# Filter rotation and first filter DFT in plain float32, in a recurrence and long-convolution kernel

## The chip, the cores and the metric

The kernel runs on one core of a Trainium2 chip. The time is that of one execution on the device, in microseconds (us); lower is better. TensorE (PE) multiplies matrices, VectorE (DVE) and ScalarE (ACT) read its results from PSUM, GpSimd (POOL) works on SBUF alone, and SyncE (SP) issues all DMAs. PEld stands for PE's weight loads.

## The reference

Two stages follow each other: a gated recurrence along the sequence, and a block that convolves with a filter through Fourier transforms. B is 4, S is 6272, D is 256, all in float32.

```python
sig = 1.0 / (1.0 + np.exp(-f_logit))
f = lower_bound + (1.0 - lower_bound) * sig
for t in range(S):
    h = f[:, t] * h + (1.0 - f[:, t]) * x[:, t]
    y[:, t] = h
proj = y @ w_proj                                  # [B, S, 3 D]
x1, x2, x3 = proj[..., :D], proj[..., D:2 * D], proj[..., 2 * D:]
H = np.fft.rfft(filter_fft, n=S, axis=0)[None]
x2_conv = np.fft.irfft(np.fft.rfft(x2, n=S, axis=1) * H, n=S, axis=1)
out = (x1 * x2_conv * x3) @ w_out
```

## The kernel before

S is split as 128 x 49 (M and Q), so that a transform along the sequence is two rounds of matmuls with small tables: a first DFT over the 128 positions of one residue, and a second one over the 49 residues. Before that, each of the 49 rows r of the sequence has to be turned cyclically by its own number of positions. For the batches this comes with the projection; for the filter it is done with matmuls against a shifted identity ("rotation").

The preparation, which `prepare` records, has these steps for the filter:

- `ff` (line 622): 13 loads of up to four rows (512 KB each), 7 into X2, the others into Hu and HA.
- `fr` (line 631): for the groups not in PLAIN = (0, 2, 4, 6, 8, 10), a copy on ACT or POOL that rounds the group to float32r, PE's fast form of float32, into one of the two buffers `afs` (the second is Hx).
- `rot` (line 639, matmul on line 637): each row times the shifted identity `rot`. Groups in PLAIN are rotated as plain float32 where they landed, with the identity read as float32; the others as float32r from the buffer.
- `f2` (line 640): the eviction of a group of rotated rows to the tile f2, in float32r, by ACT or DVE (lines 291 and 296 of the helper `copy`).
- `FF1` (line 663, matmul on line 661): the first DFT. A unit is 8 columns of pairs of channels, 16 units in all; each column is one matmul with 128 x 128 of f2 as weights and the table D1r as the moving operand. D1r is stored twice side by side, so that a matmul moves 256 columns in float32r, of which half are not used. A unit is two steps of four matmuls.
- `afs` (line 666): the eviction of half a unit, 512 elements per partition, to one of two buffers. `mX` (line 670) copies its first column.
- `FF2` (line 681, matmul on line 679): the second DFT of a unit; `hw` (line 684) evicts the spectrum, `hst` (line 688) stores it to DRAM, from where each batch loads it back (`H`, line 772).

All of FF1 needs all of f2. `hgrn` for batch 0 runs between the steps of the filter: loads of f_logit and x in 13 chunks (`load`, line 334, through four sets of buffers), sigmoid (`sig`, 337) on ACT, a product (`u`, 339) on POOL, transposes (`su`, 353, on line 351) on PE, a gate (`f`, 364 or 366) and the scan (372) on DVE. A chunk has two `su`, one for each half of the channels, and its buffers are free for the chunk four places later once both are done.

Then, for each batch: the projection to the convolved part (`P`, line 725), the first and second DFT (737 and 795), products with the spectrum (816 and 825), the inverse (835 and 869), the gates x1 and x3 (400) and the output projection (887). The next batch's recurrence runs between these steps.

Nothing is scheduled at run time. Every step is recorded with the tags that it reads and writes and a cost that a planner used offline; the string ORDER then gives, for each step in turn, its engine and its PSUM bank, and `emit` issues them in this order. So each engine, and SP's queue of DMAs, has a fixed sequence, and an instruction that waits holds back all behind it on its engine. WARM steps are matmuls without use of their result (two of float16 with 256 columns each, line 603), which fill gaps of PE.

Of the kernel before, what the change touches and what calls it, by code (L numbers as in the profile page):

```python
# [64 lines left out]
class Plan:  # L65
# [68 lines left out]
    "EuACnQEaMEkWCZYCbCEvYCoIClUElGCjSE6AEmOEoQFMgCmECiYE7YEpIFNgCkCEwUEqICwWExEE0SCxGEyMCqQFXgETYE1CC1WErgCpYCrAEPYFWg"
    "E2KE8UEbYCNgFEAE/QC2OC3SFhgFAAFFYE9MCuWFggC4CCdgFBICvGAGgFOACzWE+MFGSCyYC0GC5YFPYFJQFHKC+UFqgFKAFIKEngC6WC/EFrgC7G"
    "FQUFLICtgDASFYADHWFRMAnRDBCFTQFSMDIGDCYDFSFZYF0gFUADQWB8gDGCFVIDDUFiAC9gDKSDEMFaQDRGDJYFjYDLCDXWFbIDVUALADNgDOSDYO"
    "DWEF1gFcIDPCFdWD7YFsADTUMTgDSYFeOCcgFkQDUEFtYDgSFfOFlAFnUDhCFmIDeWMfgFoEC8gDaSD3YDfGCMgFpMFuQEDYDbCMggDlWDZYCsgEfY"
    "F2AFvIDMgDnUDiYDmGEzYF+gDjSFwIDoEBtYFxWDkCE3YJQUFyODqQDpYJSEF3YFzOJRVDrAEHYJVSJWTJTFDsgF4QF7WJYDF5IDtgDuUJUYF8OJXC"
    "F6IF/gMUgJaTF9OGigJbQJZYJcDGIRJdIG0gDvEGQWJeYGJBG9gGUUGRGGGQDdgGVEGKSGHIMhAGAWGLCGOQGBOGMUGPAGrgGCSDcgGNEMrgGEQGDK"
    "MVAGSWGFAGWSGTOJfVGXCJgXJkRJlQJhFJmJGYTJnAJivGeVGZDJoYJpQJjYGfNJqXJuRJsHGaSJrIJwBGjWGbCJtYGcUGnuJvRGdEJzTJxpJ0QGoY"  # L140
    "J1DJ4XJyYJ2IGgSGsUJ6HGhKJ3YG1QGwEGluJ5XG5AHGSGkYJ7vGxYGmYJ9VHQgHHCJ+RGusJ8YGpWJ/FHMSGvYGqGG3oGtYHZgG+UG2YG6YKABHIW"
    "HNKG4YGyQHJGHAsHKSGzAKBYHigG7WHLCMsgHCsHBYKCQG/YMiYKEAHORHRTHDYHrgHPJMtAKDQHVrHERHTDKHVKFoG8GHWYHUYKITHFJKGYKMQKJF"
    "HaWKOAKKrH0UHeuKLYH4QHSYH+gH1EHbYHXSHcuHfYMuYHjUHYCHlsH5AHdYIHgH2WHgSH3GHnsHmYHkYHsQMWYHhCH6WHuoHoYIQgHpUH7GH/SHwo"
    "HvYHqEH8WKNQIBCH9OIIUHxYHtYIZgIDqIAYIRRIKEICYHyWITBKPoIEYKRTHzGIMsKQYKSUIiQKTDILYIsgIFWINYIjAKUsKWTIVpKVYKXVIGGMXQ"
    "IJYI1gKZFIUYKYLIWYIaWMYAMbUIeGMZIIOSM3gMcEM4gKbXISYIPCIfYMdMIXQKdHImSIYAIcuMjUInCIkQKaYMkMIdYJHgIoWIlAI+gKcTMlMIbY"
    "KgSIpGItQKerKiCIqUMnWIvoKfYIxAKhTNDgMoGIyYIgRIrMNEgIwYM5AMpOKlQI2UIhBKjrMvWI3YKnAIuYI6sKkYMzSM6YMwGKmRNQgI4EMxOKqQ"
    "I7YNPgM0CIzUKsAM1KM7WI0EJAYI5YNFAKrUKopKvSKtsKpYM8GM/QKuYKxCJIUNGYM9ONbgNAAI8SNcgJMEMygNBIKwXJKEK0WI9CI/UJLYKyvK2G"
    "K1RJBsKzYNHSK3BNRAK5WJDsJCYK4YNLQNICNlgK7OJEYJFUNMANSYNmgNJKK6XJGEK+WNdANNIK/SNTTJJYLAGNeYK8vNXQNUDLBqK9YLDVNvgNYA"
    "NVLLEWLCYNwgLFFLIXLKHLJVJNYLGuNnANfSLLtLHYLNWNZILMYLOXLPGNiUNgCLQvN5gJOQNjENhKLRYNoYNOgRtXJPAN6gRuWM+gNkMRvHLSQRwG"
    "LXSNxALTINpUNsWNqENyYLYKLUQODgNtGOEgNrMLZSLVAMeYNuOLcULWgLaCNaYNzQLdMLbgRyXN0ALhSR0HN1IN7AN2ULmWONgN3ELiKN8YOOgLeQ"  # L150
    "OFAN4MLjSLfALnOOGYLrULkCN9QLsMOAWN+ALoSMqAOXgN/IOYgOBGLlgOHULpCNKgOCOLwQOPAOKSLxILtWUwgOLCOQYLqgOIEOMKLyQLuGOJMLzA"
    "L1WORSOZAL2OL0gRzROSCOaYLvgL6UR1BNWYOTKOUQMaYObWM2YU8gL7MOVAL3SOcGNCAOdOOeUMmAOWIVJgL8WL4CVIgUxgOfMMEQL9GU9gOgML/S"
    "LggMFIOxUL5gL+gMAKOhQOyEOtWOiAOvTOuOUyAO3QOwDOjWO4AOnTUzYOkOVKAO1QOoDOpWO2AOlUU+AOzQOmMOrSU/YO0AMBUOsKOqGMJQMCEVLY"
    "O5WMKIO9SMDgO6GMGUO+CMOQPDWMPIMHEPHuO7QRxYR3SO8AO/UPFuPIYR2YR4TPAEMLQR5KPGYPtgR6DPBUPLWMMAR7YPCMPbSPNuPTUPdCPEYR8Q"
    "PXEPMYPPuPOYPJRR+APlVPKBPYYPVsPQYP2gR9QSBXPmFPRRR/oPWYSDHPjVSAYPfqPSBPcYSCQPUYPeYSGXSEASHUPgYSIPPkFPpSPnQSJsPZWPoA"
    "SFYQIgPqKSKYP/gPuUPaGPhQPysPrSP3WPiAPsKPzYSLVPwsP5GP4YQRQPvYSNFP6YQJSQSAP7uPxYQbgQAVMIgSMUQEFSQQP8YSOsQNCP0WQkgSSI"
    "SPYSRUP1GQCtQFYSVQSWTSXAQTWSTsQDYP9QQUGSYrSUYQBYSaVQtgQLqSZYQOYQVTP+AMNgQGWScFQWLQMYSbSQHGQcQQKYQ2gSdCQXUQgoQPWSeY"
    "QYESfTQeoQhYQQGQZRQlUShDQaJQfYRJgQ3WQnsQpEQdYQ/QQmYQ7GQiSQqYQ5GRAIQoYQuUQjCU0WQysQwERBQQvYU1GQxYU4SQzYRCAU2OQrUVUg"
    "RSgU5CVAQVVgQsEQ6YU6KQ0WRbgVBARDUQ1GSgSVCISkTREEQ8YRKWSiqSlQSmDROuSjYSpRSnARFUSrBSqQSoYRMuRPYRGESuTVERSsoQ4YRNYSwD"
    "RHUVggSvWRIMVFBStYSzXVhgSxGRTTRkgVGJVWAQ9VSyYRVLVMQQ+FRLYRXrVXYS0TS1HRQVVNAS2rRYYS4SRRFVOIS5XS3YS9US6CRWYRcVS/ES7v"  # L160
    "VQSReFRgtS8YVYQVsgVRCVtgS+XViARUYVSKRhYTCWRfYRZUVZATAvTDTRaETHSVaITBYTIXTEGVjYVcUTJCTFrRlQV4gVdETKvTGYTMWV5gRpARno"
    "TNTTLYU7gTOGRmYTRXRdYRqYTSSTTHVeMRoYVkQVuARiWTPrVlATWUTUqTQYVvYRjGTXTVmITVYTbSTYEVoWTdCVngTcRVpOTZDWCgVwUV6ATaYVqO"
    "WDgTgQRrSVxETepTiAVrYV0WVyMRsCTfYV7YThQWMgV1GTlRTjoTmVTnBMQSV2OTkYToFTqUTrRMRCTpYTsEMSgTvSU3ATtpWNgV8UVPYWEATuYTwK"
# [814 lines left out]
```

## Time and profile before

| | |
|---|---|
| median of 3 runs | 460.49 us (459.06 to 460.7) |
| the profiled execution | 461.27 us, span 459.3 us |
| PE busy | 444.2 us (97%), 6009 matmuls |
| DVE, ACT, POOL busy | 402.4, 406.7, 306.0 us |
| DMA | 121.40 MB, mean 264 GB/s |
| mean granted PE clock | 0.999 |

The busy time of an engine is the time in which at least one of its instructions ran. Matmuls follow each other in a pipeline, so the mean duration of one (0.2 to 0.4 us) is longer than the distance from one start to the next. In rows in order of time, "x8" is a number of instructions, the first number the start and the second the length of the merged piece, in us from the start of the span; what is in brackets is idle time before it and what ended it. SPq rows are the issues of DMAs. Rows of lines 291, 293, 296 and 298 are evictions by the helper `copy`, to be told apart by their tiles.

### The profile page before, as it was taken

To read this page: it belongs to the slowest core of one execution; us is meant where nothing else is said; L and a number is where in the kernel's file an instruction comes from. 1 tells how busy PE (TensorE), PEld (TensorE's weight loads), DVE (VectorE), ACT (ScalarE), POOL (GpSimd) and SP (SyncE) were. 2 spreads that over 40 slices of the span, in tenths; PEclk is the share of its full clock that TensorE was granted. 3 is DMA by queue.
4 is the path that set the end of the run, shared out by engine and by line. 5 is a ranking of instruction groups with operands and counts; after the bars stand their busy time and mean duration, and the time that the engine had idled before them with its cause. 6 is when DMAs were issued, how large, how long until landed. Compare 5 with 4: busy or idle time off the path is not lost.

```text
span 459.3 us, 14604 instructions
## 1 busy us (share of the span) xinstructions
PE 444.2 (97%) x6009; PEld 346.6 (75%) x6009; DVE 402.4 (88%) x450; ACT 406.7 (89%) x563; POOL 306.0 (67%) x282
## 2 busy tenths in 40 slices
...
GB/s 321 387 349 330 316 340 407 314 143 253 272 310 248 337 326 298 106 233 265 279 229 296 284 294 350 101 320 326 226 244 304 287 229 26 241 185 186 31 289 290
DMA packets 45154, 121.40 MB, mean 264 GB/s; under 512 B 4384, under 2 KB 8352, under 8 KB 45088
## 3 DMA queue, kind: packets, MB, share of 16 engines
...
HBM read 86.12 MB, written 31.98 MB: 257 GB/s over the span
## 4 chain that ended last, share of the span: by engine, by line
PE 66%; DVE 15%; ACT 6%; DMA 5%; issue 5%; POOL 2%; ACTq 0%; SPq 0%; DVEq 0%; POOLq 0%
PE PS L400 15%; PE PS L725 9%; PE PS L835 9%; PE PS L887 7%; PE PS L351 6%; DVE HA L372 6%; PE PS L795 6%; PE PS L737 6%; DVE ys L875 4%; DMA FL<-in_f_logit_dram 3%; PE PS L869 2%; PE PS L661 2%; DVE PP L816 2%; DMA X<-in_moe_filter_fft_dram 1%; ACT fTs L364 1%
## 5 line engine op out<-in xcount | busy, mean ns | idle before, releaser
L339 POOL TENSOR_TENSOR XT<-XT,FL 128x1024 f32<-128x1024 f32 (+1 forms) x49 | 109.8, 2245 | 53.6 <-ACT FL L337 36.5
L372 DVE TENSOR_TENSOR_SCAN HA<-fTs,HA,PS 128x512 f16<-128x512 f32 (+1 forms) x96 | 112.9, 1201 | 2.8 <-ACT fTs L364 2.0
L400 PE MATMUL PS<-HA,W 128*128 128x490 f16 (+1 forms) x416 | 103.8, 367 | 1.0 <-DVE HA L372 0.3
L825 POOL TENSOR_TENSOR PP<-HA,Hu 98x1008 f16<-98x1008 f16 x39 | 81.8, 2106 | 6.8 <-ACT HA L291 2.7
L291 ACT CAST HA<-PS 128x1024 f16<-128x1024 f32 (+1 forms) x98 | 79.1, 833 | 4.2 <-PE PS L737 2.2
L431 POOL TENSOR_TENSOR zt<-gx 128x490 f16<-128x490 f32 (+1 forms) x43 | 52.4, 1223 | 41.1 <-ACT gx L291 16.6
L816 DVE TENSOR_TENSOR PP<-PS,Hu 98x1008 f16<-98x1008 f32 x57 | 66.7, 1199 | 0.6 <-ACT gx L293 0.5
L875 DVE TENSOR_TENSOR ys<-PS,zt 128x1024 fp32r<-128x1024 f32 (+1 forms) x52 | 58.7, 1149 | 8.5 <-PE PS L869 6.7
L887 PE MATMUL PS<-Wo,ys 128*128 128x256 f32 x392 | 58.1, 293 | 0.6 <-DVE ys L875 0.3
L364 ACT ACTIVATE fTs<-PS,cc 128x512 f32<-128x512 f32 (+1 forms) x84 | 55.3, 679 | 2.8 <-PE PS L351 2.1
L835 PEld LDWEIGHTS <-PP 98*128 98x128 f16 x1024 | 50.2, 97 | 9.8 <-issue 1.7
L400 PEld LDWEIGHTS <-W 128*128 128x128 f16 x416 | 34.4, 97 | 30.6 <-issue 7.8
L835 PE MATMUL PS<-VV,PP 98*128 98x98 f16 x1024 | 55.9, 206 | 0.3
L887 PEld LDWEIGHTS PS<-Wo,ys 128*128 128x128 f32 x392 | 49.7, 188 | 6.0 <-DVE ys L875 1.5
L293 ACT ACTIVATE gx<-PS 128x490 f32<-128x490 f32 (+1 forms) x87 | 50.1, 583 | 4.5 <-PE PS L400 3.1
L291 ACT CAST Th<-PS 128x784 f16<-128x784 f32 x59 | 48.4, 820 | 4.1 <-PE PS L835 3.1
L337 ACT ACTIVATE FL<-FL 128x1024 f32<-128x1024 f32 (+1 forms) x49 | 49.4, 1010 | 1.8 <-DMA FL<-in_f_logit_dram 1.6
L351 PE MATMUL PS<-iden,FL 64*128 64x64 f32 x736 | 42.7, 231 | 2.5 <-ACT HA L293 0.9
L725 PE MATMUL PS<-W,HA 128*128 128x256 f16 x392 | 44.6, 273 | 0.2
L725 PEld LDWEIGHTS <-HA 128*128 128x128 f16 x392 | 43.0, 142 | 1.2 <-issue 0.2
L351 PEld LDWEIGHTS PS<-iden,FL 64*128 64x128 f32 x736 | 31.7, 138 | 16.0 <-issue 2.6
L422 DVE TENSOR_TENSOR zt<-PS,gx 128x490 f16<-128x490 f32 (+1 forms) x61 | 38.8, 647 | 1.6 <-PE PS L400 0.9
(128 smaller groups left out, 741.8 us busy)
## 6 DMA issues: line engine op xcount, KB each, us to landing
...
```

What stands on the lines that cost most here:

```text
L291: nc.scalar.copy(dst, src)
L339: op("u", {"POOL": 0.1 + 0.553 * nb}, lambda e, xt=xt, ft=ft: nc.gpsimd.tensor_tensor(xt, xt, ft, op=AOP.mult), r=[("ft", k)], w=[("xt", k)])
L351: nc.tensor.transpose(bank(pb)[:, at[p] + j:at[p] + hn:nb], src[ps, j, cols], iden[ps, ps])
L364: nc.scalar.activation(fT, sT, AF.Identity, scale=by, bias=1.0)
L372: nc.vector.tensor_tensor_scan(h, fT, bank(pb)[:, 512 - hn:512 + hn], init, op0=AOP.mult, op1=AOP.add),
L400: nc.tensor.matmul(PS[:, p, 0:n], W13[:, kh, js], HA[:, HB[kh] + t0:HB[kh] + t0 + n], start=(kh == 0), stop=(kh == 1))
L725: nc.tensor.matmul(pp[:, r - r0, :], column(HB[kh], q_of(r)), W2[:, kh, :], start=(kh == 0), stop=(kh == 1))
L816: nc.vector.tensor_tensor(pr, px.unsqueeze(1).broadcast_to([TB, 2, UE, 63]), hh, op=AOP.mult)
L825: nc.gpsimd.tensor_tensor(pr, spec[:, o, :, 1:64].unsqueeze(1).broadcast_to([TB, 2, UE, 63]), hh, op=AOP.mult)
L835: nc.tensor.matmul(PS[:, ib + o, pr * TB:(pr + 1) * TB], PP[:TB, k, o, n, 2 * pr:2 * pr + 2, :], v[:TB], start=(n == 0), stop=(n == 1))
L875: nc.vector.tensor_tensor(late["ys"][:, yk, :, 0:rn * 128], PS[:, cb:cb + 2, 0:rn * 128], late["zt"][:].rearrange("p k r m -> p k (r m)") ...
L887: nc.tensor.matmul(po[:, i, :], late["ys"][:, yk, kh, i * 128:(i + 1) * 128], Wo[:, kh, :], start=(kh == 0), stop=(kh == 1))
```

## The change

- PLAIN and the seven `fr` copies are gone. Every group of the filter is rotated where its load put it, with both operands declared plain float32; `rot` and f2 are float32 tiles instead of float32r.
- D1r is a float32 table of 128 columns, stored once. A unit of FF1 is one step of eight matmuls with 128 columns, both operands plain float32, and one eviction of 1024 elements per partition; FF2 and mX of a unit wait for that one.
- The planner's costs for the two steps are other ones, and ORDER is a new string for the whole kernel (2371 steps instead of 2410: 7 `fr`, 16 `FF1` and 16 `afs` fewer).

The sequences that ORDER spells out, for the stretch that is edited (numbers are groups, units and chunk halves; `load` 0 is the first of f_logit):

- SP before: ff 3, 2, 0, 1, 4, 7, 6, wcol, ff 5, 12, 8, 9, 10, 11, load 0, 1, 4, 2, 3, 5, 6, 7, wl0, load 8, hst1, ... After: load 0, ff 0, wcol, ff 5, 6, 2, 4, 3, 1, 7, 8, 9, 12, 10, 11, load 1, 2, 4, 3, 5, 6, 7, wl0, load 8, ...
- PE before: 10 warm, rot 3, warm, rot 2, 0, 4, 1, 6, warm, rot 7, warm, rot 5, two warm, rot 8, 9, 10, warm, rot 11, two warm, rot 12, two warm, FF1 (halves) 1, 0, 3, 2, FF2 0, FF1 4, FF2 1, FF1 5, 6, su0, FF1 7, su1, ...
- PE after: 11 warm, rot 0, four warm, rot 2, 6, 4, 5, 1, two warm, rot 3, 7, 8, 9, 10, 11, warm, rot 12, warm, FF1 0, 1, FF2 0, FF1 2, FF2 1, su0, FF1 3, su1, FF2 2, FF2 3, su2, ...
- `afs` evictions: 23 on ACT and 9 on DVE before; 12 on ACT and 4 on DVE after.
- From the first P on, PE has the same steps in both, in a similar sequence. Some evictions and short copies of the batches change between ACT, DVE, POOL and SP.

```diff
-PLAIN = (0, 2, 4, 6, 8, 10)
 ORDER = (
...
-    FF1 = [("FF1", u, h) for u in range(NU) for h in range(2)]
+    FF1 = [("FF1", u) for u in range(NU)]
...
-        rot = tmp.tile([128, 256], F32R, name="rot")
+        rot = tmp.tile([128, 256], F32, name="rot")
...
-        D1r = tmp.tile([128, 2, 128], F32R, name="D1r")
+        D1r = tmp.tile([128, 128], F32, name="D1r")
...
-        f2 = head.tile([128, NEP * PF + 16], F32R, name="f2")
+        f2 = head.tile([128, NEP * PF + 16], F32, name="f2")
...
-            if g in PLAIN:
-                fr, ft, turner = raw, et, rot[:].bitcast(F32)
-            else:
-                j = g // 2 % 2
-                fr, ft, turner = afs[j].rearrange("m r i k -> m (r i k)").rearrange(
-                    "m (r d) -> m r d", d=D), [("af", j, 0), ("af", j, 1)], rot
-                op("fr", {"ACT": 0.08 + 0.214 * rn, "POOL": 0.1 + 0.235 * rn, "DVE": 0.1 + 0.267 * rn},
-                   lambda e, raw=raw, fr=fr, rn=rn: copy(e, fr[:, 0:rn], raw[:, 0:rn]), r=et, w=ft)
-
-            def rotate(e, pb, r0=r0, rn=rn, fr=fr, turner=turner):
+            def rotate(e, pb, r0=r0, rn=rn, raw=raw):
                 pr = PS[:, pb:pb + 2].rearrange("m a (r e) -> m (a r) e", e=256)
                 for r in range(r0, r0 + rn):
-                    nc.tensor.matmul(pr[:, r - r0, :], turner[:, m0_of(r):m0_of(r) + 128],
-                                     fr[:, r - r0, :], start=True, stop=True)
-            rt = op("rot", {"PE": (0.43 if g in PLAIN else 0.12) * rn}, rotate, r=ft + ["rot"], take=2)
+                    nc.tensor.matmul(pr[:, r - r0, :], rot[:, m0_of(r):m0_of(r) + 128],
+                                     raw[:, r - r0, :], start=True, stop=True)
+            rt = op("rot", {"PE": 0.216 * rn}, rotate, r=et + ["rot"], take=2)
...
-            for h in range(2):
-
-                def first(e, pb, f=f2, j=u * UE + h * 4):
-                    pa = PS[:, pb:pb + 2].rearrange("m a (i c) -> m (a i) c", c=256)
-                    for i in range(4):
-                        nc.tensor.matmul(pa[:, i, :], f[:, (j + i) * PF:(j + i) * PF + 128],
-                                         D1r[:].rearrange("m x k -> m (x k)"), start=True, stop=True)
-                f1 = op("FF1", {"PE": 0.475}, first,
...
-                op("afs", either(512), lambda e, pb, af=af, h=h: copy(
...
+            def first(e, pb, f=f2, j=u * UE):
+                pa = PS[:, pb:pb + 2].rearrange("m a (i c) -> m (a i) c", c=128)
+                for i in range(UE):
+                    nc.tensor.matmul(pa[:, i, :], f[:, (j + i) * PF:(j + i) * PF + 128],
+                                     D1r[:], start=True, stop=True)
+            f1 = op("FF1", {"PE": 0.9}, first,
+                    r=[("f2", g) for g in range(13)] + ["D1r", "f2e"], w=[("FF1", u)], take=2)
+            op("afs", either(1024), lambda e, pb, af=af: copy(
+                e, af, PS[:, pb:pb + 2].rearrange("p a (i r k) -> p r (a i) k", r=2, k=64)),
+               w=[("af", u % 2)], src=f1)
```

More of the change, by code (lines that the diff above doesn't have):

```diff
@@ L134 @@
[L134 to L163, printed above, removed]
@@ L189 @@
[L189 to L192 removed]
+    "AAYDJgA+gAMYABIAiQACIADgAxWBNgAuSBQgAkWAZQBEgAnUBKgA9YANIAaQBHgAyQAmVAfWAcUA/QBBgDLAAEYBTgAqTBWgAtXAgSBZgAlTAPIAOA"
@@ new lines @@
+    "BFSBAAATYAVYBRVBigBGCBcgBLQBSFBOTBMABCWARIApQBfgBDGAhQBPLBIRDKgDVgBJBASIDhgBUTDWgBXWBVLDigBaQDtgBYGAUIDugBdSBbAAWY"
+    "BeKAFgBgUAXYAbRBhEBjWAjRBkOAQABnQDMYBsSBoABtKBqWBzUBpYBrOAYYDXABvQDNSB0MDjAB4WBuYDYYDOCBwIDRUB5GD5gDPKB2QDSED6gB7W"
+    "B3ADkYDTMDZSB8GAeRAdRDaKAsQDvADdWDbKB1YDlQEFgDeGDwYEGgB/SDfODmAAIADpUCACDnICEWERgB6YD7AESgDqMAoRDoYAGgArTCCQCFGCBY"
+    "DrMDxSCDACGYDyKD8YD1UEHACLQDzKEbgEcgAHAAvXD2MCHWCMAEIYD3MCIGD9QEBSD+IETACQUElgCNYD/IEmgECCEUYEJWCREEDKENQEKGCOUEwg"
+    "AKAEOIEvgCTSCSYCPEBlYCJgELOCUCCcUEPIEdAEVSCdMEYQEWCEeYCXWE5gEnAEZIE6gCKgEXKCYGEfUEoYAJAEaICaWEgEEiSCbGEhMCfQFEgFDg"
@@ new lines @@
+    "CgACZYEpWBxgCeYEjKCjUExACigEkKDsgCoQCkEChgEyYEqOCpACmSErOEsUE7ACrQFOgEtMD0YC0WFNgCsAClYEuMBygCqYE8YCnCEzQC1OEAgE0A"
+    "E2SFFAE1ICvULsgE3CFGYDUgE9QCwEE4KFAWALACyUL5gFBOC7SCWgCzECxYE+IC2YL4gBmYB9gE/IC8CFHUB+gEMYLtgFPAC3SFCOFIEDAQCtgC4C"
+    "FJMDgYFXgFKWDBAFQYC6gC+SFLOD4YAwUC/CIpUDQYFMODDQC9YIrEEEYIqSDEAIuVDCYDcYIsqIvUIwFItYEQYFRWFUQDHSFSOMEgFVAFTOFYgIzV"
+    "DICFWII0WIxsFbQGWgI2GI1NIyYDGgFtWMFgFcADFgFhSCVgFuGFpUFiKF7gL6AFrWC5gLuAL7YFjSFsOCugFqEFnQFkKI4XI3YGNgFZUI6HFoIFlS"
+    "FaEFdWFmKMGAFfQFeOGEgFvTFgAI5XFwDI9RI7vI+QJCSI8YJAAFxWJEKI/BF3UFyOJDQJBYF4EFzRJHTJFoF0BF8WJGYF1UGAuJJDJISF2EJMTJKq"
@@ new lines @@
+    "JNRGBYJODJRXF+uJLYJPBGFUJTHF5SGOQJQYF/YGpgF6KGJEJSWGSIGfSF9YJUuGGYJWVGKYGgCGHsJXRJVYGCWJYFGlSGIYGDGGQoGXUGTYGygJZB"
+    "GhWGmKGRYGLQGiGGZsGjSGMAGPYG7gJaYGUWGkCGbsGaYJbQGYYJdAGnRGqTGcYHEgGoJGVGJcQGsLJgRJeoJhXGtYGdSGurJfYJjHJiBJlQGeCGzW"
+    "GvYJnIGrYHXgHNUG0YG1uJkYGwSHOEHRQG3uG2YLvYGxCG8UHSAHAsG4YHggHPWG5SHQGG+sHBYHFQG9YHGYG6CMHYHTWHHoG/YHpgHCUHUGHYSHJo"
+    "HIYHDEHVWJmQHaCHqUHWOHKYHygJooHhRHbYHsEHcqJpYHLWHjBH7QHMGHlpHdYJqTHZYIFgJrUHkYJsDHeWHmYH8AJtsJvTHusJuYJwSHfGLwQHiY"
+    "IOgJyCHrYJxLHtYHzWHvYLxAL0UH3GLyIHnSMQgL1EMRgJ0XHoCJzYIXgL2MHwQJ2HH/SHxAH4YH1uL8UIACH9QL9MH2YIBWH+AJ1SL+MH0YIggJ5T"
@@ new lines @@
+    "ICGIGQJ3qJ7DIDUMAWIIoJ4YIKAJ6TMcgMBGILYH5RMdgIEMIJYMSAMCOIPUH6BJ+QJ8rMIWIHYKAAMTYITsJ9YMMSMJGJ/RMogIREMKOKDQIUYMpg"
+    "MNCIMUKFAISYMOKMUWINEKEQMVGKBpMYUMeAKGoKCYKISM0gIQYIZYMWOKHYM1gIhQMZEMfYKJTKKCMaMIlAIVWIjAIWGKLrIYUIkYMqAKMYMgSIcs"
+    "MkQMhCIasM+gIdYKNVMlAM/gMrYKOWKPFKSXMiKIbYIeUKUHM2AKTXKQuKXSKVvKRYImYIfEKYTMmIKWYMsWKZCKcVMtGKarMwQM3YKeFMuOKbYKdU"
+    "NIgMxAKhVNJgKiTKjFKfsKmXNAAKnWKkrKgYMjYM4UMyIKlYKoHIiYM7SNBYM5ENTgKpGInQM6MNSgM8CMngRGWIoARHXM9KKqYRJHKrQRIGNCUKsI"
+    "NKAKwSNFWNDEKxKNLYKtQNcgNGGNdgNEMKySKuANHOK1UKzCKvgNMQK2MK0gRLWNNAK6SRNGNOINUANPUK/WNmgNQEK7KNVYNngK3QNeALzgMvgNRM"
@@ new lines @@
+    "K8SK4ALAONfYLEUK9CK5gNWQLFMNZSNXALBWNwgNaCNYINxgMzgNgULCGNbKLJQNoANjWLKILGSUJgNhENpYL/gNkGNiMLLQLHCNlOLMALOSMLYNqU"
+    "L3YLPKLNgLTQNrEMDYMXgRMXNyANsMNtSROHNzYUWgNuCN0WLUIUVgLQUN1GMPAN2OMbYLVQLRENvKN3ULWALdWUhgN4MLYSN5MUKgULALeOUigOKU"
+    "K+gOIQLSgLZKOLELIgN6WLXgOJALDgOGTN7OUXAOQQOHLUYYOEWORAN8UOFOOMQN9EOASONIUjAOOUOBCUkYOCWOPEN+SODOLaUN/CUMYLiWLbEOSS"
+    "LjOOWQLcgOTCLfUOXILnSLgEOcWLoKOUQOeuRKYRQSOVAOYUOguRRTRPYOfYOZELkQRTLOhYPGgRSCOaUOkWLlAObMO0SOmuOdYOsURUYO2CRVQOwE"
+    "OouOnYOiRRXAO+VOjBOtYOusOpYPPgRWXOlYOxYRaQO/FOqRRYvOvYRcAO8VRZYO4qOrBRbQO3YPYgRfUO9FRdoRgXO5YPCSRhMReYRiHPAQOyWO1Y"
@@ new lines @@
+    "PBAPhgPDKRjYPHUOzGO6QPLsPESPQWO7APFKPMYRkVPJsPSGPRYPqQPIYRmFPTYPiSPrAPUuPKYP0gPZVLhgRlUPdFRpQPVYRnsPmCPNWP9gRrARoY"
+    "RqTPOGPbtPeYRuRRvURwBPsWRsrPcYPWQRxsPtGRtYPaYRzVQGgRyYPkqPnYPuTPXAPfWPvDR1NPlYP1QPgGPwSP5oPjYQPgR0VPxCPoWR2tP6YR4T"
+    "PpGP3oR3YPyRP+UR6DQQWPzJP4YQCEQigQAsQYQP2YQUGQDYP7SQSGQZIQBYQHUP8CUNWQJEQLsQaQP/YQIYUOGQKYURSQbAUPOQMYQEUUtgUugUSC"
+    "UZQQrgQFEQTYUTKQNWQ0gUaAQcUQOGR5SUbIR9TQdEQVYQjWR7qR+QR/DQnuR8YSCRSAAQeUSEBSDSSBYQluQoYQfESHXUdQSFqQRYQmYSJHQgVU5g"
+    "SIUQhNUeASGYSMSU6gSKsSNXUvAQ9gUfIQWVSLYSOCQsTQtYQXFSPvQkYUlRUwYQwrQuDSQYQpWUmBSRTQqGQxYUnJSSUSWQSTDQvYQ1WSYASUsUpS"
@@ new lines @@
+    "Q3GQ5uSVYSXVVFgUqCUxQVGgU7AQ4YSZtQ6YSbWUrKSaYQyUUyASdGScXUzISgTQzEU8YShSSiDU1USevSjCQ+QVRgSfYU2ESlTUsgRAoQ2YSmSVSg"
+    "SkYSnDQ7WRCASoqRBYSqTQ8GRDYU3MSpYU9RSsDVBWVHAU+JSrVVcgSvUVbgU/JQ/YVCGSwQVIYS0TSyASttRERSxEVDOSuYS2DS1VVTAVJTSzYS3t"
+    "VNWRFBVKLS4YS5QVlgVUYVAALmgS6SVLLS7AS+RVmgS/VVOGUQgS8qTDTTBFVPOS9YTABLpUTFDTEQTCYLqETISTGoVdAVVUTHYTJKTNQUoAVeYVYW"
+    "VWETOITKSVwgVZGVvgVXMTPQTLCVMYVaOU4YTSUTQATMgVfSVnATTMTXWViQVgCVoYTYOTUUV5gVjAV6gTRgVhKTZWTVELrgVkIVEYVpUTaGTcSVqE"
+    "ZjWTdKVxAVsQZkXWDgVrMVtATeSVyYWEgZmHVuIZlGThUTfCTmWTiMVzQV7AU0YTggZoTTnOTjUV0AV8YZqDV1ITrWTkEV2STsOWNgToUV3CWOgWFA"
@@ new lines @@
+    "V4KV9QTpETwWWGYWASTxOV+ATqgTtUWBCcmgV/IWHWUcYTuEVQYWCKZpRWIGUUYTvgT1UWPATWgUgYWJOWKSZrBWQYcygWLCWRQT2MczgTyWWSAWMK"
+    "T3UTzGWTIWUWT/Sc+gT4EWVOT6QWWOTlgUAKcngWlWT0gTbgT7IWmGWtTT5gc/gWjWWuDWrRWkOc0AWXUWsBc1YWnWWYMdAAWpSWoOWhQWqCWfUWiA"
+    "WZWWgMcoAWbQWaOcpYWdSWcIT8UWeCUEQT9EWxSUFIWvWZnYWyCW1QWwOWzUW2AdBYZtTZuSW0MZvDUBWZwqW3QW5UUCGZxYW4IcqSW9sW6YW7EXBQ"
+    "ZsYcrCXbWXFoW+YZyVXcGXCYZzUW8YZ0NXGYZ3RZ1EXDoXJWZ5BcuUXNGZ2YXjgcsKXEYXLGW/QXsgcvEZ4WXOYXAAZ8XcwMZ9TZ+HXHQZ6uXZUXIA"
+    "Z/rZ7YXMYc2WXaMaAYc6Sc3GaBRdWgc7Cc4OXdUaDBXSYX1gaCQXKYXeEdKgaGRc8KdLgXRWaEAXfUXTuaIBaFYXPSXgEaHRXVuXUYaLQXQCdCUaNA"
@@ new lines @@
+    "aJJXWYX+gXhSXkWdDEXiKaKYXXQXmGdEMX2SXYAXlYaMWXnYXouX6CXtQX4CYJUaOGXxoXpYdGSYKEaPYXqWdigXvoXyYdHCYRgaQRdjgXuYXrGaRV"
+    "X5YdIKXwYYagaVUaSBT+gXzWaXEaTtYHQdMAX0OaUYX/UX7YYIAYNSYBsA2XaWXYOCaaQYDsYCYabRYAYYjgX3YdJAYLSdNYadBaYvYEYYsgX8UYMC"
+    "acIctgaZYYFWdXgX9MdkAYPQYSSaeYYQIY1UYGGYWqYbQY2EdlYafWYUqYXYagTahGakVaiDalUYdoYVYY/gamFdOWUDgYTYanEajYYkSYfoYeYdPG"
+    "apQYmCYYUaoYdQOYgYZIgarAY3RcxgYZEaqQYcYYoqYnYY4BYhWY5UdYAYiOYpYauRYtSasoawBYlYZRgdZYavWY6EYxqatYYqQaxGY7UYvqYyYYrA"
+    "ZAWY8EYuYZCuYwYayYZagazSa0Qa1CYzUZEuZDYa2AdSSY0Ea3YY9QZFYZJWdvgdTCY+IZbUdugZNOZBYa4RZKYZdEdUKa5QZOYa6Ba9XZfEa+RZLu"
@@ new lines @@
+    "a/HZGSa7AZSUbApZHCZMYa8YdaWZUsbBYZWEdeQdbGZXYbCVd5gZVYZPSdcOd4gbEFdfAbDUbHVZQCdgIbIXZcYZeYbMWbJFdmSbFsdqQbKvdnCbGY"
+    "bNUeDgbOGZTYbLYdoKZgYbRVeCgdrAZYWdhgbTFbPsbSTZZGbWVbQYbUrbXSdwAdsIbVYbbTZhWbYFdxYbdDbZqbcRZiGbgQbepbaYUGUbhSbiAbfY"
+    "UHMd6AblWbjqUIgdyQdFYbkYbmOd1Ud7YdzAiATeMgd2Ed0IiBSdRgbnWeNgiDCd3MiCDbqQboGd8SbrIbvUeEAd/WbwMd9CbsQeWgeFYeAGbpgd+K"
+    "eXgA0UbtAbxUeBObugb0SdtYbyEb5Qb1KeGWeOAeJUb6Ib2SePYeggeKEehgeHGeLMbzgAzRb3Cb+QeIOeYAeQUeTSb/IeZYb7WeREeqgddgeUCerg"
+    "eSMcAQb8GeVKA1VcBAcDUcIWeiAcEMeaQedSebAejYcJOiFUeeCiGViHEecIcFWiIFdVYefKcNQcGGekUcOIcHgenWelEc5gcKSeoGemMdpAcSQesA"
@@ new lines @@
+    "cLCcPUetYcTIc9AcMgeuSepOcCgcUQevCcQEewKexWcRgeyOcXSezOb9gccUcYKb4gfEWcVAcdMe4SfFGcWgfIQe5Ce6UfJAe2ScZWe3Ce0Qe7EcaO"
+    "fGSe1Acbge8VfHCfAQe9NfKSfBAchWfLCfCQciOiEYe+VfDIiKUiJYe/FcjSiLQckKiPRiMEclgfMSiNAiRJfOUfNCiOYfQQfPMfSWfRAfWSiQUfTG"
+    "faqiUViSEfUQfeWfYqfbYiWFfmTiTYiVVfoDfVIfZYgAgiZSfiOfXYiaTibCiXtfcQfjYicriYYieVfdAfqridYfuSifQfwCfnYfguijXfrYffYigF"
+    "fpYf2RilHikUihofhYf3BgJgfkWimsiiYioQflGfyqinYfxYf4UipRf5Ef6WfzYirJf8SiqAitVgbgf7Gf9KiuUisYgSgfsQiwEivNf+SfvYgBWftA"
+    "f/KgKUixYgFugkSgOEf0QglCgCYgDugGYiyXgLYizVf1AgPYi0PgEYi3Tgugi4WgMsi5DgHQi6Gi1tgTSgNYgIAg3ggUYi7YgcWi2YgVKgmUggGgXq"
@@ L193 @@
+    "kPAkXMkbSkUGkYUkcKkVgkQgkgWkZEklQkhOkdSkagkiWkeCkmIkqUkjGkfgkvQkrMknSkkgksWkoCkwIk0UktGkpgkxRk1Mkugk5WkyBk2Uk6Okzg"
+    "A7Qk3Ek7Qk4gA8Uk8IA6WA5Uk+Vk/Nk9gA4WlATlBLlCg"
 )
```

52 lines of the change are left out of this document (9 added, 43 removed).

## The prediction

> **What bounds the kernel now.** I read the page's busy times first, then a table by stretches, then TensorE (PE) in order of time up to the first batch's projection. Columns of the stretches: length, busy us (x instructions) of PE, PEld, DVE, ACT, POOL, then granted clock, DMA share, GB/s.
>
> ```profile
> span 459.3 us, 14604 instructions
> PE 444.2 (97%) x6009; PEld 346.6 (75%) x6009; DVE 402.4 (88%) x450; ACT 406.7 (89%) x563; POOL 306.0 (67%) x282
> 0.00:23.60 23.60, 21.05 (x113) 16.46 (x113) 14.67 (x44) 17.33 (x18) 10.67 (x27) 1.00 0.93 355
> 23.60:75.30 51.70, 48.96 (x618) 38.36 (x619) 47.40 (x51) 50.48 (x73) 44.43 (x53) 1.00 0.95 342
> 75.30:130.00 54.70, 53.76 (x723) 41.34 (x721) 46.91 (x51) 51.06 (x70) 37.12 (x33) 1.00 0.78 267
> 150.00:200.00 50.00, 49.41 (x696) 42.44 (x696) 42.50 (x43) 46.44 (x59) 29.18 (x23) 1.00 0.73 257
> 300.00:350.00 50.00, 49.93 (x749) 35.80 (x748) 49.27 (x54) 47.83 (x75) 41.61 (x37) 1.00 0.86 276
> ```
>
> PE is the tightest engine, 97% over the span and 98 to 100% in every stretch shown after 75.3 us. What comes later there comes later at the end. The change works before that: stage 1 (to 23.6 us: filter loads and rotations, with warming matmuls between them) and stage 2 (23.6 to 75.3 us: filter DFT mixed with the first batch's recurrence), where PE has 51.70 - 48.96 = 2.7 us idle and ACT, DVE and DMA are nearly as full. The clock is granted in full, so durations can be carried over.
>
> The prices that decide are those of matmuls. In order of time, start, duration, what; the first five rows are merged pieces of the PE timeline, the next five pieces of the chain that ended last, which run to the start of the next piece:
>
> ```profile
> 6.83 5.35 PE L637 MATMUL PS<-X,rot 128*128 128x256 f32 x24
> 16.23 0.73 PE L637 MATMUL PS<-afs,rot 128*128 128x256 f32 x4
> 19.64 1.89 PE L637 MATMUL PS<-X,rot 128*128 128x256 f32 x8
> 87.69 1.07 PE L737 MATMUL PS<-D,X 128*128 128x128 f16 x16
> 89.83 0.61 PE L737 MATMUL PS<-D,X 128*128 128x128 f16 x8
> ...
> 25.96 0.68 PE PS L679 x4
> 26.64 0.66 PE PS L661 x4
> 27.96 1.14 PE PS L661 x8
> 29.10 0.66 PE PS L351 x16
> 75.32 10.70 PE PS L725 x98
> ```
>
> Read the counts against the code. A plain float32 group (X,rot) rotates four rows with four matmul calls, but its row has x8: the three groups rot2, rot0, rot4 stand as x24. A rounded group (afs,rot) has x4. So a plain float32 matmul is two instructions, and each is slow: (5.35 - 1.89) / 16 = 0.216 us from one start to the next. A float32r matmul of 256 columns (L661) is one instruction of (1.14 - 0.66) / 4 = 0.12 us, and each run of them has 0.66 - 4 x 0.12 = 0.18 us on top. A float16 one of 256 columns (L725) takes 10.70 / 98 = 0.109. One plain matmul of 256 columns thus costs 0.432, four times the float16 one. The plan's costs in the diff (0.216 a row for the rotation, 0.9 for a unit of FF1) are right only if there were one such instruction for each matmul; the rows say two.
>
> **Stage 1, the rotation.** 25 rows go from float32r to plain: a group of four from about 0.66 to 8 x 0.216 = 1.73 us. All 49 rows come to 49 x 0.432 = 21.2 us; before, 24 x 0.432 + 25 x 0.12 = 13.4. In 23.6 us before the first FF1 that fits only if rotations start early and run back to back. When they can start is read from the copies that wait on the loads, and from the queue's issues, each of which stands until the load eight places before it has landed:
>
> ```profile
> 4.92 1.05 ACT L291 CAST Hx<-X 128x1024 fp32r<-128x1024 f32 x1 [2.90 <-DMA X<-in_moe_filter_fft_dram]
> 8.78 1.04 POOL L303 CAST afs<-X 128x1024 fp32r<-128x1024 f32 x1 [2.92 <-DMA X<-in_moe_filter_fft_dram]
> 12.62 0.33 SPq L334 DMA_DIRECT2D FL<-in_f_logit_dram  x1
> 13.69 0.33 SPq L334 DMA_DIRECT2D XT<-in_x_dram  x1
> 15.00 0.80 SPq L334 DMA_DIRECT2D FL<-in_f_logit_dram  x2
> 20.43 0.33 SPq L334 DMA_DIRECT2D gx<-in_x_dram  x1
> 23.66 2.30 PE L661 MATMUL PS<-D1r,f 128*128 128x256 f32 x16
> 30.88 0.33 SPq L334 DMA_DIRECT2D FL<-in_f_logit_dram  x1
> 22.32 1.17 ACT L291 CAST f<-PS 128x1024 fp32r<-128x1024 f32 x1
> ```
>
> The first load (group 3) is there at 4.9 us and the fourth (group 1) at 8.75: 1.28 us each. 12.62, 13.69 and 15.00 are the landings of group 6, wcol and group 5, so the tiny wcol costs 1.1 us. The new queue is load0, group 0, wcol, groups 5, 6, 2, ...: 4.9, 6.2, 7.3, 8.6, 9.9, 11.1. The new PE order is rot0, four warming ops, rot2, rot6, ...; rot2 waits for the last of these. From 11.1: eleven groups 11 x 1.73 = 19.0, rot12 0.4, four warming ops (two float16 matmuls each) 8 x 0.109 = 0.9: 31.4 us, and with group 11's eviction (1.17, from the row at 22.32, begun before rot12) FF1 starts at 31.9. Before, 23.66: **+8.2 us**. Loading does not cover it: group 11, the last, had landed by 20.43, when the issue eight places after it went out; one load more ahead makes that about 21.7. If wcol costs nothing and half of the warming fits into waits, +6.5; if rot2's load lands a slot later, +9.5.
>
> The seven rounding copies go, and the evictions change; of both, rows of each size (x count | busy, mean ns | idle before):
>
> ```profile
> L291 ACT CAST Hx<-X 128x1024 fp32r<-128x1024 f32 x2 | 2.1, 1046 | 3.0 <-DMA X<-in_moe_filter_fft_dram 2.9
> L303 POOL CAST afs<-X 128x1024 fp32r<-128x1024 f32 x2 | 2.1, 1042 | 3.0 <-DMA X<-in_moe_filter_fft_dram 2.9
> L291 ACT CAST afs<-PS 128x512 fp32r<-128x512 f32 x12 | 6.9, 588 | 0.1
> L296 DVE CAST Hx<-PS 128x512 fp32r<-128x512 f32 x5 | 3.4, 676 | 0.3 <-PE PS L661 0.2
> L296 DVE CAST f<-PS 128x1024 fp32r<-128x1024 f32 x3 | 3.7, 1225 | 6.9 <-ACT f L291 4.8 <-PE PS L637 2.1
> ```
>
> The copies, six of about 1.04 us and a short one on ACT and POOL, are worth nothing here: each stood between a load and its rotation, and the rotations, not the copies, now end last.
>
> **Stage 2, the first DFT.** Before, 128 instructions in 20 runs (counted in the PE timeline): 128 x 0.12 + 20 x 0.18 = 19.0 us. After, 16 units x 8 matmuls x 2 instructions = 256 of 128 columns, in 14 runs by the new order. No row has a plain float32 matmul of 128 columns. By columns alone it is half of 0.216, 0.108; if loading its 128 x 128 float32 weights sets the pace, it is more. These rows bear on that (min/median/max ns):
>
> ```profile
> L637 PEld LDWEIGHTS PS<-X,rot x40: 186/190/192, 6.7 to 20.9; 128*128 128x128 f32 x40
> L661 PEld LDWEIGHTS PS<-D1r,f x128: 186/188/193, 23.6 to 69.2; 128*128 128x128 f32 x128
> ```
>
> A plain load shows 190 ns, a float32r load 188, and float32r matmuls with such loads follow each other at 0.12, a little over the 0.109 of float16 with equally many columns. So I take 0.12, the float32r row being nearest. The ends are 0.108 and 0.216 (no gain from fewer columns, were plain loads what sets 0.216). Even the float16 rows of 128 columns, (1.07 - 0.61) / 8 = 0.058 each, would leave 256 x 0.058 + 14 x 0.18 = 17.4, hardly under today's 19.0. With 0.12: 256 x 0.12 + 14 x 0.18 = 33.2, so **+14.2 us of PE work**. The 2.7 us in which PE waits now can take some of it, as ACT and DVE get ahead: **+11.5 us** for the stage.
>
> The Trainium skill weighs against a term here: "TensorE: Matmul & The Clock Gate", section "Step-by-step: what each phase is for", says the next weights load while the current matmul runs, and its section "Wait — 56ns, not 53.3ns?" gives 55.6 ns for 128 columns; with the four passes that "FP8 and Floating Point Precision" (section "TensorE Precision Notes") gives true FP32, a matmul would be 0.222 us instead of 0.24, and by that estimate the prediction would be 2.3 us lower. The trace agrees with four passes (0.432 against 0.109) but not with a fully hidden load (0.12 against 0.109).
>
> What goes with it: 32 evictions of 512 columns become 16 of 1024. On ACT 23 x 0.588 = 13.5 becomes 12 x 1.17 = 14.0, on DVE 9 x 0.676 = 6.1 becomes 4 x 1.225 = 4.9. Both cost nothing while PE is late, and would cost their difference if ACT were again the fullest. FF2, mX and a unit's two buffers now wait for a whole unit's eviction, up to 0.6 us later; the new order has another unit or a transposition between FF1 and its FF2, so I take nothing, at most 16 x 0.2 = 3 us. The smaller D1r copy is off the path.
>
> The load queue: load8 is behind the second transposition (su1), at 30.88 before. After, FF1 0 to 2, FF2 0 and 1, su0, FF1 3 and su1 come to 4 x 2.1 + 2 x 0.68 (L679) + 2 x 0.66 (L351) = 11.1 us on PE: 43.0. SP is idle meanwhile, and all later loads, wraps and spectrum stores follow behind. Before, 75.3 - 30.9 = 44.4 us were enough from there; 43.0 + 44.4 = 87.4 lies before the new end of the stage, 31.9 + 51.7 + 11.5 = 95.1. DMA is hidden.
>
> **After 75.3 us** the same PE instructions run in a like order; copies change between ACT and DVE. PE has under 1 us idle in each stretch shown, so the new order can win or lose some 2 us: 0.
>
> **Sum.** The profiled execution took 461.27 us (459.3 of span, 2.0 around it), 0.78 over the median 460.49. 461.27 + 8.2 + 11.5 = 481.0; against the median 480.2, so 480.
>
> **Rivals.**
> - *Partly absorbed.* Stage 2 was as much ACT's (50.48 of 51.70) and DMA's (0.95) as PE's, so more of the PE work may fit in. Price: 0.108 a matmul (256 x 0.108 + 2.5 = 30.1, +11.1), 5 us taken up by waits that busy pieces hide, +6.5 in stage 1: +12.6, 473. Against it: PE's 48.96 busy leaves 2.7.
> - *The load sets the pace.* At 0.216: 256 x 0.216 + 2.5 = 57.8, +38.8 - 2.7 + 8.2 = +44, 505. Against it: the two load rows.
> - *Faster: the pair runs as one.* If the second instruction cost nothing with a moving tensor of half the columns, and in the rotation when both tiles are declared float32, the plan's prices hold: a rotation group 0.87 against 1.28 for its load, so stage 1 is the loads' again (21.7 + 0.87 + 1.2 = 23.8, +0.1); FF1 at 17.4 saves 1.6, and the lighter evictions about 0.7: 458.3. It decides as soon as a unit of FF1 is under 1.2 us. Against it: x24 in 5.35 us, for the same instruction on the same types.
> - *The order gains it back.* It would need 19 us, and PE has 15 idle in the whole span (459.3 - 444.2). Left out.
>
> **How the numbers follow.** My case 0.78 (474 to 488), absorbed 0.10, load-paced 0.05, faster 0.05, another small change 0.02. The range 469 to 491 holds my case, the absorbed one, and stalls of the order; load-paced and faster are left out with half of the tails. A difference under about 0.5% can't be told from none: slower 0.93, within 0.03, faster 0.04 (458.3 is at the edge of it).
>
> **What would show it.** Right: every L637 group has x8 and 1.73 us; FF1 (the L661 group) has x256 in pieces of x16 over about 2.1 us; the first of them starts near 32 us, the first projection (L725) near 94; afterwards the stretches look as before. Wrong: a rotation group below 1 us, FF1 under 1.3 a unit or over 3, or DVE or ACT, not PE, ending last in stage 2.

## Result and profile after

The changed kernel takes 485.36 us (median of 4 runs, 483.67 to 486.51), the kernel before 460.6 in the same comparison (459.06 to 461.87). The ratio is 1.0536, 95% interval 1.0491 to 1.0581: slower by 24.8 us, inside the predicted range and 5.4 over the predicted time.

The page after and the stretches, with the columns of those before, cut where the first FF1 (34.2 us; before 23.66) and the first projection (98.3 us; before 75.2) start:

```profile
span 484.5 us, 14847 instructions
PE 465.6 (96%) x6162; PEld 367.9 (76%) x6162; DVE 407.4 (84%) x453; ACT 399.4 (82%) x541; POOL 301.4 (62%) x276
...
34.10:98.40 64.30, 61.03 (x747) 50.82 (x747) 48.11 (x48) 49.50 (x60) 38.47 (x42) 1.00 0.75 256
98.40:153.10 54.70, 53.98 (x723) 41.44 (x723) 49.15 (x54) 48.81 (x69) 36.37 (x32) 1.00 0.76 253
323.10:373.10 50.00, 49.73 (x740) 35.18 (x739) 49.02 (x53) 48.21 (x76) 42.95 (x38) 1.00 0.82 281
```

Stage 2 has 61.03 us of PE work in 64.30; before it was 48.96 in 51.70. DVE and ACT do about what they did and now have room, and the share of DMA falls from 0.95 to 0.75. PE's idle time in the stage is not used up: 3.3 us against 2.7. Later stretches look as before. The profiled execution is the longest of the four (486.51 us). With the starts of FF1 and of the projection as cuts, of its 25.2 us more of span, 10.5 came in stage 1 (34.19 for 23.66), 12.6 in stage 2 (64.14 for 51.50) and 2.1 in all that follows (386.2 for 384.1).

PE's timeline after shows the prices (start, duration), the by-line view gives min/median/max ns, and the last three rows are stretches of 2 us:

```profile
5.92 1.97 PE L626 MATMUL PS<-X,rot 128*128 128x256 f32 x8
7.72 1.04 PE L601 MATMUL PS<-iden 128*128 128x256 f16 x8
11.29 10.59 PE L626 MATMUL PS<-X,rot 128*128 128x256 f32 x40 [2.53 <-DMA X<-in_moe_filter_fft_dram]
22.15 1.89 PE L626 MATMUL PS<-X,rot 128*128 128x256 f32 x8
34.19 3.81 PE L648 MATMUL PS<-D1r,f 128*128 128x128 f32 x32 [0.64 <-DVE f L294]
38.58 2.05 PE L648 MATMUL PS<-D1r,f 128*128 128x128 f32 x16
...
L648 PEld LDWEIGHTS PS<-D1r,f x256: 186/192/192, 34.2 to 92.4; 128*128 128x128 f32 x128
...
10.00:12.00 2.00, 0.71 (x3) 0.66 (x4) 1.03 (x3) 0.00 (x0) 2.00 (x4) 1.00 1.03 422
12.00:14.00 2.00, 2.00 (x7) 1.61 (x7) 0.00 (x0) 0.00 (x0) 0.42 (x1) 0.60 1.03 420
14.00:16.00 2.00, 2.00 (x7) 1.60 (x6) 0.00 (x0) 1.14 (x1) 0.00 (x0) 0.54 1.02 412
```

Every rotation group has x8; a unit of FF1 has x16 and takes 2.05 us, two take 3.81, so one instruction comes (3.81 - 2.05) / 16 = 0.11 after another. The five groups from 11.29 should take 8.64 + 0.16 = 8.80 (40 distances of 0.216, and the end of the last) and take 10.59, 1.8 us more: after PE had waited 2.53 us for group 2's load, the granted clock is half from 12.4 to 15.8 us, and starts that lie 0.216 us apart elsewhere lie 0.427 apart there.

### The profile page after: what moved, and what is told of

Same layout as the page of the kernel before. It is cut to its first block, busy times and chain, and to the rows that moved or that the text cites. A ratio compares the mean times of both kernels' runs of the same rounds, so it can differ in the third digit from the quotient of the medians.

```text
span 484.5 us, 14847 instructions
## 1 busy us (share of the span) xinstructions
PE 465.6 (96%) x6162; PEld 367.9 (76%) x6162; DVE 407.4 (84%) x453; ACT 399.4 (82%) x541; POOL 301.4 (62%) x276
## 4 chain that ended last, share of the span: by engine, by line
PE 70%; DVE 10%; ACT 6%; issue 5%; DMA 4%; POOL 3%; SPq 1%; DVEq 0%; ACTq 0%; POOLq 0%
PE PS L398 14%; PE PS L710 9%; PE PS L872 8%; PE PS L820 7%; PE PS L349 6%; PE PS L648 6%; PE PS L722 5%; PE PS L780 5%; PE PS L626 4%; PE PS L854 4%; DVE HA L370 3%; DVE PP L801 2%; DVE ys L860 2%; DMA XT<-in_x_dram 2%; DMA X<-in_moe_filter_fft_dram 2%
## 5 line engine op out<-in xcount | busy, mean ns | idle before, releaser
L289 ACT CAST HA<-PS 128x1024 f16<-128x1024 f32 (+1 forms) x92 | 75.4, 841 | 5.6 <-PE PS L722 2.5
L429 POOL TENSOR_TENSOR zt<-gx 128x490 f16<-128x490 f32 (+1 forms) x40 | 48.5, 1216 | 36.2 <-DVE ys L860 17.0
L291 ACT ACTIVATE gx<-PS 128x490 f32<-128x490 f32 (+1 forms) x90 | 51.7, 583 | 3.8 <-PE PS L398 3.6
L420 DVE TENSOR_TENSOR zt<-PS,gx 128x490 f16<-128x490 f32 (+1 forms) x64 | 40.8, 647 | 2.5 <-PE PS L398 1.5
```

Source lines behind the costliest of these rows:

```text
L289: nc.scalar.copy(dst, src)
```

## Experiments

The theory at this point: the time is PE's added instructions, one to one, in two separate parts (rotation, FF1), and a half clock on top. The rivals: part of it is the new order, or the two parts lengthen each other.

**One part each, and one instruction a matmul.** The hybrids take the loads, the rotation and the order of one kernel up to the first FF1, and FF1 and the order of the other from there.

```diff
 h1_rot_as_before: rotation, loads and order of before; from FF1 on the change
+            if g in PLAIN:
+                fr, ft, turner = raw, et, rot[:].bitcast(F32)
+            else:
+                op("fr", ...
 h3_rot_alone: the reverse (all groups plain; FF1 and the order of before from there)
 h2_ff1_float32r: h1 with, and e1_new_rot_ff1_float32r: the change with
-        D1r = tmp.tile([128, 128], F32, name="D1r")
+        D1r = tmp.tile([128, 128], F32R, name="D1r")
-        f2 = head.tile([128, NEP * PF + 16], F32, name="f2")
+        f2 = head.tile([128, NEP * PF + 16], F32R, name="f2")
```

> The changed kernel with its rotation undone: loads, rounding copies, groups and order of the kernel before up to the first FF1, then the plain float32 FF1 in the new order. Theory (PE's added time comes one to one): FF1 starts at 23.7 us again instead of 34.2, stage 2 stays at 64.3 us, so about 485.4 - 10.5 = 474.9. Rival (the late start of stage 2 also starves it, since loads and rotations collide there): stage 2 gets shorter too, to 60 or less, and the time is under 471. Rival (the rotation is hidden anyway): 482 or more.

> The kernel before with only the rotation of the change: all groups plain float32, no rounding copies, loads and order of the change up to the first FF1; FF1 in float32r with 256 columns in halves and the order of before from there. Theory: FF1 starts at about 34 us, stage 2 takes its 51.7, so 460.5 + 10.5 = 471. Rival (part of the rotation's delay is taken up in stage 2, since loads of the batch are then there already and POOL and ACT have been waiting): 466 or less.

> The changed kernel with FF1 in float32r instead of plain float32, nothing else: same order, same evictions, 128 columns. Theory: 485.4 less the 12.6 us by which stage 2 grew, 471 to 474. Rival (the order, not the matmuls): 480 or more.

Measured: h1 474.62 us (ratio 1.0295, 1.0268 to 1.0323), h3 471.66 (1.0233, 1.0171 to 1.0294), e1 472.56 (1.0284, 1.0213 to 1.0355), with 461.16 for the kernel before. FF1 with the new order behind it costs 13.5 us, the rotation alone 10.5 (its four executions lie between 468.8 and 474.2, so the interval allows 7.9 to 13.6); together 24.0, against the 24.8 of the change. So within that interval they add, and neither hides the other. In h1 stage 2 takes 64.1 us although it starts at 24.3; in h3 it takes 51.8 although it starts at 33.6. e1 shows that the new order and the single eviction do not make stage 2 long by themselves: with one instruction a matmul, it is 51.3 us, as before (51.5), in the same order in which it took 64.1. Its stretch, and its FF1 beside that of h1, both with 128 columns:

```profile
34.10:85.40 51.30, 47.33 (x618) 36.74 (x619) 47.13 (x48) 48.66 (x60) 38.33 (x42) 1.00 0.85 302
...
L648 PE MATMUL PS<-D1r,f x128: 271/275/330, 34.1 to 79.6; 128*128 128x128 f32 x128
```

```profile
24.20:88.40 64.20, 60.77 (x745) 50.63 (x745) 48.07 (x48) 49.94 (x60) 42.27 (x50) 1.00 0.85 290
...
L655 PE MATMUL PS<-D1r,f x256: 275/275/378, 24.3 to 82.6; 128*128 128x128 f32 x128
```

13.44 us of PE's busy time are between them (60.77 - 47.33), and 12.9 of the stage.

> Rotation of the kernel before, and FF1 in the shape of the change (one step of eight matmuls of 128 columns, one eviction of 1024 a unit, new order), but in float32r: one instruction a matmul. Theory: a unit of FF1 takes 8 x 0.112 to 0.12 + 0.18 = 1.1 us instead of 2.0, stage 2 falls from 64.3 to 49 to 52 us, and the time is 458 to 462. Rival (the new order or the single eviction is what made stage 2 long): stage 2 stays over 58 us, 468 or more.

Measured: 466.55 us (1.0118, 1.0086 to 1.015), a miss of both. Stage 2 took 55.5 us. Its stretches name the reason: PE was busy for 2.13 of 3.40 us just after FF1 had begun, and then for 10.2 us the clock was at half:

```profile
24.80:28.20 3.40, 2.13 (x18) 1.65 (x17) 1.29 (x2) 3.06 (x4) 3.40 (x8) 1.00 1.02 408
28.20:38.40 10.20, 10.20 (x82) 8.42 (x82) 6.82 (x7) 6.34 (x8) 8.33 (x8) 0.50 0.57 211
```

The joined order had put ACT's sigmoid and its table load ahead of the first eviction of FF1, for which the first FF2 waits. A second try moves that sigmoid behind it (one step of ORDER):

> As the run with the rotation of before and FF1 in float32r (466.55), but ACT evicts the first unit of FF1 before its first sigmoid, which with its table load stood between (the joined order put it there). Theory (in that run the new order cost nothing; 1.3 us of idle before the first FF2 had the clock at 0.5 from 28.2 to 38.5 us, and that made stage 2 55.5 us): the clock stays full, stage 2 takes 51.4 us, 462. Rival (the new order costs 4 us in stage 2 by itself): 466 again, at full clock.

Measured: 466.71 us (1.0129, 1.0105 to 1.0152), stage 2 54.3. The sigmoid, now late, made POOL's product late, for which the first transposition of x waited 1.97 us; the clock was at half again, this time from 32.4 to 35.8 us. Neither h2 nor h2b tells the cost of the order at full clock; e1, whose start of stage 2 is that of the new order, does for float32r.

**The half clock.** Two ways to close PE's wait before group 2:

```diff
 e6_warm_through_wait
-            for k in range(2):
+            for k in range(8 if i in (17, 20, 7, 12) else 2):
 e7_group2_loaded_early: SP order in ORDER
-  load 0, ff 0, wcol, ff 5, ff 6, ff 2, ff 4, ...
+  load 0, ff 0, ff 2, ff 6, wcol, ff 5, ff 4, ...
```

> The changed kernel, with the four warming steps between rot0 and rot2 made of eight matmuls each instead of two, so that PE works through the wait for group 2's load (2.53 us of idle, 8.8 to 11.3). Theory (that idle is why the granted clock was 0.5 from 12.4 to 15.8 us): the clock stays full, eight instructions of the rotation take 0.216 us each again instead of 0.427, FF1 starts 1.7 us earlier, 483.5. Rival (the half clock is a fixed start-up effect, or the load ends last anyway): same start of FF1, 485.

> The changed kernel with only the load queue altered: groups 2 and 6 are loaded before wcol and group 5, in the order in which PE rotates them. Theory (stage 1 is rotations from the first one whose load stands late): no wait of 2.53 us and no half clock, FF1 at about 29.8 us instead of 34.2, so 481. Rival (later loads end last, at 26.8 us for group 11): FF1 stays at 33 or later, 484 or more.

Measured: e6 484.02 us (1.0498, 1.048 to 1.0515), e7 481.63 (1.0443, 1.0427 to 1.0458), the kernel before at 461.22. e6's FF1 starts at 32.70, e7's at 29.90, where the change's starts at 34.19. The first row is the five groups in e6, the second in e7:

```profile
11.48 8.90 PE L626 MATMUL PS<-X,rot 128*128 128x256 f32 x40
```

```profile
8.47 9.12 PE L623 MATMUL PS<-X,rot 128*128 128x256 f32 x40
```

Both are at full clock; e6 gives no data earlier and so wins 1.5 us, by keeping PE busy with matmuls of no use. e7 needs none of that and wins 4.3 us of the start, because rotations, not loads, end stage 1. Stage 2 stays at 64.1 in both. The half clock does not come in every execution of the change: 3.41 us of it lower the mean granted clock by 0.0035, and three of the four have 0.995 or 0.996, but the one of 483.67 us has 0.999. That one is as fast as e6, whose four lie between 483.75 and 484.13.

**What sets FF1's pace.** e9 halves the columns of the plain matmul; half of each spectrum is then not computed.

```diff
-                    nc.tensor.matmul(pa[:, i, :], f[:, (j + i) * PF:(j + i) * PF + 128],
-                                     D1r[:], start=True, stop=True)
+                    nc.tensor.matmul(pa[:, i, 0:64], f[:, (j + i) * PF:(j + i) * PF + 128],
+                                     D1r[:, 0:64], start=True, stop=True)
```

> The changed kernel with plain float32 FF1 matmuls of 64 columns instead of 128 (half of the table left out, so half of each spectrum isn't computed); everything else the same. If loading the weights sets FF1's pace: start to start stays at 0.11 us, and the time at 485. If the columns set it: 0.06 us, FF1 takes 1.1 us a unit and the time falls to about 472.

Measured: 482.17 us in its one run; stage 2 63.4, for 64.1 in the change. The first two units:

```profile
32.11 3.76 PE L648 MATMUL PS<-D1r,f 128*128 128x64 f32 x32 [0.64 <-DVE f L294]
...
L648 PEld LDWEIGHTS PS<-D1r,f x256: 186/192/192, 32.1 to 89.6; 128*128 128x128 f32 x128
```

3.76 us with 64 columns, 3.81 with 128: columns do not matter there, and from start to start both are at 0.112 us. e1's float32r with 128 columns is at 0.112 too. What they share is the 128 x 128 float32 weights, loaded once for each instruction, so the load is the likely pace-setter. No run changes the weights alone, so an equal fixed cost of a float32 instruction is not ruled out. Of the 4.3 us that e9's one execution is shorter than the change's profiled one (486.51), 2.1 lie in stage 1, where FF1 starts at 32.11: the two kernels are the same there, but e9's wait was 1.85 us, and the clock stayed full.

**FF1 in the old order.** e5 has only FF1 plain (halves and evictions of 512 kept), e8 only the 128 columns, e10 only float16.

```diff
 e5: D1r and f2 F32;   e8: F32R as before;   e10: F16;   in all three
-                        nc.tensor.matmul(pa[:, i, :], f[:, (j + i) * PF:(j + i) * PF + 128],
-                                         D1r[:].rearrange("m x k -> m (x k)"), start=True, stop=True)
+                        nc.tensor.matmul(pa[:, i, 0:128], f[:, (j + i) * PF:(j + i) * PF + 128],
+                                         D1r[:, 0], start=True, stop=True)
```

> The kernel before with one edit: FF1 in plain float32, two instructions of 128 columns a matmul, still in halves of four, with the old order and the old evictions of 512. Theory (PE's added instructions come one to one, whatever the order): 128 more of 0.112 us, less 128 x 0.006 for those that were 0.118, so stage 2 goes from 51.5 to about 65 and the time to 461.2 + 13.5 = 474 to 475. Rival (in the old order, made for a PE with waits left, part is absorbed): 471 or less.

> The kernel before with one edit: FF1's float32r matmuls move 128 columns instead of 256 (the second half of the table wasn't used). If loading the weights sets the pace (0.112 us with 128 columns against 0.118 with 256): PE saves 128 x 0.006 = 0.8 us and half a streaming time at the end of each run (20 x 0.05 = 1.0), ACT is as full as before: 459.5 to 461. If the columns set it: 0.06 us a matmul, PE saves 7 us, ACT's 50.5 us of work keep stage 2 at 50 or more, 459 to 460.

> The kernel before with FF1 in float16: f2 and the table in float16, 128 columns a matmul, evicted from PSUM as before. Its float16 rows of 128 columns follow each other at 0.056 us, so PE does about 128 x (0.118 - 0.056) + 20 x 0.05 = 9 us less in stage 2. If PE alone bound stage 2 before: 51.5 to 43 us, 452. If the evictions did as well (ACT busy 50.5 of 51.7 us, DVE 47.4): stage 2 stays at 49.5 to 51.5 us, 459 to 461, and what is added to PE there costs more than what is taken from it gives.

Measured: e5 472.36 us (1.0249, 1.0225 to 1.0274), between theory and rival: stage 2 63.1, some 2 us less than expected. h1 has the same rotation and the same FF1 instructions and takes 2.3 us more (474.62), with stage 2 at 64.1: this is what the new order from FF1 on and the single evictions cost with plain FF1; which of the two was not tried, and the intervals of the two ratios just overlap. e8 460.8 (0.9995, 0.9978 to 1.0012): no difference that can be measured; it paces at 0.113. e10 459.81 (0.9974, 0.9962 to 0.9986), the only version that is faster than the kernel before, by 1.1 us. Its stretch of stage 2 and its FF1:

```profile
23.20:74.00 50.80, 42.42 (x624) 30.19 (x623) 47.78 (x53) 49.96 (x75) 44.70 (x53) 1.00 0.96 351
...
L661 PEld LDWEIGHTS <-f x128: 95/98/100, 24.1 to 67.8; 128*128 128x128 f16 x128
```

The load of float16 weights stands at 98 ns where the float32 ones stand at 190, and e10's FF1 instructions follow each other at 0.056 us. PE's busy time falls from 48.96 to 42.42 in these stretches, and the stage, by its own cuts, only from 51.5 to 49.4. ACT, with 49.96 of 50.80, is then the fullest, and DMA has 0.96; the chain that ended last runs by turns over DVE, ACT and PE, so no single engine is shown to bound it. So stage 2 was balanced. Adding 12 us to PE costs 12, taking 6.5 away gives 2.

## Why the prediction was right, and where it was off

- *Two slow instructions for each plain matmul*: right. 0.216 us in the rotation, x8 a group, x256 in FF1; h1, h3 and e1 show that these are nearly all of the cost. The rest is the order with its evictions (h1 against e5, 2.3 us) and the half clock.
- *Stage 1, +8.2*: measured +10.5. The load of group 2 was predicted for 11.1 and its rotation began at 11.29. The term left out is the clock: 1.8 us in the five groups after the wait. My own landing times left PE a wait of some 2 us behind the four warming steps, and I said the clock could be carried over in full; e6 and e7, which close the wait, keep the full clock.
- *Stage 2, +11.5*: measured +12.6, from two errors that offset; that they nearly cancel is luck. Each instruction was taken at 0.12 and has 0.112; read from the pieces, 12 single units of 2.0 and two double ones of 3.8 come to 31.6 us, not 33.2. And 2.7 us of PE's idle time were to absorb some; in the new order none was absorbed (3.3 us idle), in the old one (e5) 1.0 (1.7 us idle). Why the two orders differ in this no run shows.
- *The Trainium skill's* 0.222 us for a matmul is nearer to the measured 0.224 than my 0.24, but not for its reason, which goes by the columns. At 128 columns these nearly coincide: half of the rotation's 0.216 is 0.108, and measured is 0.112; only the 64 columns of e9, still at 0.112, tell them apart. The Trainium skill ("TensorE: Matmul & The Clock Gate", section "Step-by-step: what each phase is for") says that the next weights load while the current matmul runs. That can hold here and still not hide the load: in e9 halving the columns leaves the pace unchanged, and so it nearly does from 0.118 to 0.112 in e1, so something longer than moving 128 columns sets it. If that is the load, the rival "the load sets the pace" had the right mechanism and the wrong bound: 0.112 and not 0.216, which the rotation has with 256 columns.
- *Evictions, copies, the load queue at nothing*: right for the copies and the queue, nearly so for the evictions. e1 has stage 2 at 51.3 with the new evictions, but with plain FF1 stage 2 is 1.1 us longer in the new order with them (h1 64.1) than in the old one (e5 63.1). h3, with no copies, starts FF1 at 33.6, nearly as late as the change; load8 went out at 44.3 (predicted 43.0) and DMA had room.
- *After the projection, 0*: +2.1 in the profiled execution (386.2 for 384.1). The other kernels in the new order have 384.6 to 386.1, those in the old one 382.5 to 383.6, one profiled execution each: some 1.5 to 2 us are the new order's. Which of its steps was not tried.
